# Routed attention and a feed-forward block on one core: 21 of the q and k sides transposed in blocks by VectorE, masks placed by transfers, small chained transfers on GpSimd's queue

## The chip, the cores and the metric

The kernel runs on one core of a Trainium2 chip. TensorE (PE in the profile) multiplies matrices and writes to PSUM, VectorE (DVE) and ScalarE (ACT) compute on SBUF and PSUM, GpSimd (POOL) computes on SBUF and can start transfers, and SyncE (SP) only starts transfers. The metric is the time of one execution on the device, in microseconds. Of the kernel before, five executions are given, with a median of 978.92 us (978.76 to 979.87).

## The reference

Attention with 4 batches, 8 heads, 768 tokens and 64 dimensions a head. Each token of q and of k is assigned to the nearest of 16 centroids of its head, and a query sees only the keys of its own cluster:

```python
q_assign = np.argmax(np.einsum('bhsd,hcd->bhsc', q_n, c_n), axis=-1)
k_assign = np.argmax(np.einsum('bhsd,hcd->bhsc', k_n, c_n), axis=-1)
mask = q_assign[:, :, :, None] == k_assign[:, :, None, :]
scores = scale * np.matmul(q, k.transpose(0, 1, 3, 2))
scores = np.where(mask, scores, -1000000000.0)
```

A softmax over the keys and a product with v follow. The heads are laid side by side into rows of 512, and a feed-forward block comes after: layer norm with a gain, a 512 x 2048 product, a ReLU, a 2048 x 512 product, and the residual. All of it is float32; the weights arrive as float64.

## The kernel before

**Two stages.** The attention stage handles 16 pairs of heads (4 batches x 4 pairs); the feed-forward stage then handles the four batches one after the other with matrix products that are split so that seven products of blocks do the work of eight. The change lies in the attention stage.

**A pair.** A pair's work on TensorE is cut into 12 steps: two halves of 384 queries (`g`) by six blocks of 128 keys (`c`). Two steps make a slot, so a pair has slots 0 to 5. For each step `scores` (L330) puts four matmuls into one PSUM tile: for each head of the pair a matmul of one-hot masks in bf16 (keys' clusters against queries' clusters, where the keys' mask holds 0 for the own cluster and -2^100 elsewhere) and one of k and q in float32. ScalarE then takes the exponential (L341). `weigh` (L353) multiplies it by v into an accumulator (L360), and VectorE adds the exponentials up for the denominators (L374, L377). Scores run a slot ahead of the weighing. There are two PSUM tiles of scores and five SBUF tiles of exponentials.

**Preparing the next pair.** q and k of the pair are loaded with 128 tokens groups on the partitions and must be turned so that the 2 x 64 dimensions lie on the partitions:

- `load` (L76) issues two transfers for a side, one per head, on SP's queue. The tiles `q` and `k` have one buffer each, so that a load starts when the one before has been transposed.
- `prep_transpose` (L236) does six 128 x 128 transposes on TensorE (L243) into two PSUM tiles, which ScalarE copies to SBUF (L249). For pair n+1 the k side is turned in slot 0 of pair n; the q side of pair n+2 is turned in slot 5 of pair n.
- `prep_sims` (L253) in slot 1: similarities to the centroids, copied by ScalarE (L269).
- `prep_turn` and `prep_route` in slot 2: three transposes, then VectorE finds the largest similarity (L285) and writes the one-hot tile (L287).
- `prep_onehot` (L297) in slot 4: six bf16 transposes (L302) into one PSUM tile whose four groups of 32 partitions are q head 0, q head 1, k head 0 and k head 1. Four ScalarE instructions copy each group to its place in `mask[n % 2][side]` (rows 0 to 31 and 64 to 95): a plain copy for q (L316), and FAR * x - FAR for k (L314). The first scores of pair n+1 use these masks in slot 5 of pair n, since scores run ahead.

**Finishing the pair before.** `finish` (L389) has three parts, in slots 1, 3 and 5. Part 0 sums the exponentials over the partitions with a matmul by ones (L397), copies the result to `dsb` (L405), and spreads each of its four rows of 384 over 32 partitions of 12 with four transfers (L407). Part 1 takes the reciprocal on VectorE (L409), stores it to `row` in DRAM (L411) and loads it back as `rb`, each row broadcast over 64 partitions (L419, two transfers that wait for the store). Part 2 multiplies x by rb (L426), stores x (L427), transposes it in 32 x 32 blocks with VectorE (L433), and stores the blocks with four transfers of 128-byte pieces (L436).

**Other work in these slots.** VectorE converts the float64 weights, seven instructions a chunk (L209 to L231): two chunks a pair up to pair 9 (split in slots 0 and 3, joined in slots 1 and 4), then one. In pairs 5 to 8 it takes row statistics of batch 0 (L464, L465), in pair 9 it finishes them, and from pair 10 it applies the norm (L493, L495).

**What sets the order.** The attention loop stands in a block whose instructions on TensorE, VectorE and ScalarE run in the order in which they are written (`manual_schedule`, L562). The order on SP and GpSimd is set by the scheduler, by when it expects each transfer to be ready; a queue issues in order, and a transfer whose input is not there holds up those behind it. In this kernel GpSimd does only memsets and one select at the start. All transfers of the attention loop are on SP.

Of the kernel before, what the change touches and what calls it, by code (L numbers as in the profile page):

```python
# [8 lines left out]
F32 = mybir.dt.float32  # L9
BF16 = mybir.dt.bfloat16  # L10
U32 = mybir.dt.uint32
I32 = mybir.dt.int32
AF = mybir.ActivationFunctionType
# [6 lines left out]
def kernel(  # L20
# [11 lines left out]
    nc = tc.nc  # L32
    B, H, S, D = q.shape
    NCL = centroids.shape[1]
    DM, FF = moe_w_ch1.shape
    P = 128
    NT = S // P
    NHALF = 2
    TH = NT // NHALF
    HC = TH * P  # L40
    Q = 32
# [4 lines left out]
    FAR = 2.0 ** 100  # L46
    WIDE = 1.0e20

    const = ctx.enter_context(tc.tile_pool(name="const", bufs=1))
# [9 lines left out]
    loads = pool("loads", 1)  # L59
    heads = pool("heads", 2)  # L60
    route = pool("route", 1)
    conv = pool("conv", 1)
    attn = pool("attn", 2)
    dram = ctx.enter_context(tc.tile_pool(name="dram", bufs=4, space=bass.MemoryType.DRAM))
# [8 lines left out]
    pairs = [(b, pr) for b in range(B) for pr in range(NPAIR)]  # L73
    loaded = {n: {} for n in range(len(pairs))}

    def load(n, names):  # L76
        if n >= len(pairs):
            return
        b, pr = pairs[n]
        for name in names:  # L80

            shape = [P, 2, NT, D] if name == "v" else [P, NT, 2, D]
            t = loads.tile(
                shape, F32, tag=name, name=f"{name}_sb", bufs=2 if name == "v" else 1
            )

            parts = 1 if n or name == "v" else NHALF
            for g in range(parts):
                cs = slice(g * NT // parts, (g + 1) * NT // parts)
                for j in range(2):  # L90
                    queue = nc.scalar if parts > 1 and j else nc.sync
                    queue.dma_start(
                        out=t[:, j] if name == "v" else t[:, cs, j, :],
                        in_={"q": q, "k": k, "v": v}[name][b, 2 * pr + j].rearrange(
                            "(p c) d -> p c d", p=P
                        )[:, cs, :],
                    )
            loaded[n][name] = t
# [24 lines left out]
    for m in mask[0] + mask[1]:  # L123
        nc.gpsimd.memset(m, 0.0)
    hits = const.tile([P, B * NPAIR], F32, name="hits")
    far = const.tile([P, 1], F32, name="far")
    nc.gpsimd.memset(far, -FAR)

    DE = HC // Q
    rdens = const.tile([P, B * NPAIR, DE], F32, name="rdens")  # L130
# [105 lines left out]
    def prep_transpose(n, side):  # L236
        src = loaded[n]["qk"[side]]
        t_sb = heads.tile([P, S], F32, tag=f"t{side}", name=f"t{side}")
        prepared[n][side] = t_sb
        for g in range(NHALF):  # L240
            t = ps("qk_ps")
            for c in range(TH):
                nc.tensor.transpose(  # L243
                    t[:, c * P : (c + 1) * P],
                    src[:, g * TH + c, :, :].rearrange("p h d -> p (h d)"),
                    ident,
                )
            if g == 0 or n:
                nc.scalar.copy(t_sb[:, g * HC : (g + 1) * HC], t[:, :HC])  # L249
            else:  # L250
                nc.vector.tensor_copy(t_sb[:, g * HC : (g + 1) * HC], t[:, :HC])
# [45 lines left out]
    def prep_onehot(n):  # L297
        t = ps("oh_ps", BF16, 1024)
        for g in range(NHALF):
            for c in range(TH):  # L300
                o = (g * TH + c) * P
                nc.tensor.transpose(  # L302
                    t[:, o : o + P],
                    onehot[:, c, g, :, :, :].rearrange("p s j d -> p (s j d)"),
                    identb,
                )

        for side in range(2):
            m = mask[n % 2][side]
            for j in range(2):  # L310
                src = t[(side * 2 + j) * Q : (side * 2 + j + 1) * Q, :S]
                dst = m[j * D : j * D + Q, :]
                if side:
                    nc.scalar.activation(dst, src, AF.Identity, bias=far[:Q], scale=FAR)  # L314
                else:
                    nc.scalar.copy(dst, src)  # L316
            prepared[n]["m", side] = m

# [69 lines left out]
    def finish(n, part):  # L390
        b, pr = pairs[n]
        if part == 0:
            den = ps("den_ps")
            for j in range(2):
                for g in range(NHALF):
                    r = (j * NHALF + g) * Q
                    nc.tensor.matmul(  # L397
                        den[r : r + Q, :HC], ones, sums[n, g][:, j, :],
                        start=True, stop=True, tile_position=(0, r),
                    )  # L400
            if n + 1 < len(pairs):
                dsb = last.tile([P, HC], F32, tag="dsb", name="dsb", bufs=1)
            else:
                dsb = late["all"][:, 1, :HC]
            nc.scalar.copy(dsb, den[:, :HC])  # L405
            for r in range(0, P, Q):
                nc.sync.dma_start(out=rdens[r : r + Q, n, :], in_=dsb[r : r + 1, :])  # L407
        elif part == 1:
            nc.vector.reciprocal(rdens[:, n, :], rdens[:, n, :])  # L409
            row = dram.tile([2, S], F32, tag="row", name="row")  # L410
            nc.sync.dma_start(  # L411
                out=row.rearrange("j (p e) -> (j p) e", e=DE), in_=rdens[:, n, :]
            )
            if n + 1 < len(pairs):
                rb = last.tile([P, S], F32, tag="rb", name="rb", bufs=1)
            else:
                rb = late["all"][:, 2]
            for j in range(2):
                nc.sync.dma_start(  # L419
                    out=rb[j * D : (j + 1) * D, :],  # L420
                    in_=row[j : j + 1, :].to_broadcast([D, S]),
                )
            late[n] = rb
        else:
            x = xs.pop(n)
            nc.vector.tensor_tensor(x, x, late.pop(n), ALU.mult)  # L426
            nc.sync.dma_start(out=xT_d[b][pr], in_=x)  # L427

            if n + 1 < len(pairs):
                y = last.tile([P, S], F32, tag="y", name="y")  # L430
            else:
                y = late["all"][:, 2]
            nc.vector.transpose(y, x)  # L433
            for i in range(P // Q):
                m = pr * P + i * Q
                nc.sync.dma_start(  # L436
                    out=x_d[b].rearrange("t (a r) m -> r (t a) m", r=Q)[:, :, m : m + Q],
                    in_=y[i * Q : (i + 1) * Q].rearrange("r (g f) -> r g f", f=Q),
                )
# [4 lines left out]
    rows = {}  # L444
# [117 lines left out]
    with tc.manual_schedule(engines=order):  # L562
        prep_transpose(0, 0)
        load(1, "q")
        turn_centroids()
        prep_transpose(0, 1)
        load(1, "k")
        prep_sims(0)
        scores(0, "qk", ("qk",))
        prep_turn(0)  # L570
        scores(1, "qk", ("qk",))
        prep_route(0)
        prep_transpose(1, 0)
        load(2, "q")
        load_weight(0)
        load_weight(1)
        prep_onehot(0)
        scores(0, "qk", ("mask", "exp"))
        scores(1, "qk", ("mask", "exp"))
        for u in range(len(pairs) * slots):  # L580
            n, slot = divmod(u, slots)
            nxt = n + 1 < len(pairs)
            if slot == 1:
                load(n + 1, "v")
            if slot == 0 and nxt:
                prep_transpose(n + 1, 1)
                load(n + 2, "k")
            if slot == 1 and nxt:
                prep_sims(n + 1)
            if slot == 2 and nxt:  # L590
                prep_turn(n + 1)
                prep_route(n + 1)
            if slot == 4 and nxt:
                prep_onehot(n + 1)
            if slot == 5 and n + 2 < len(pairs):
                prep_transpose(n + 2, 0)
                load(n + 3, "q")
            if slot == 1 and n:
                finish(n - 1, 0)
            for i in (2 * u + 2, 2 * u + 3):  # L600
                if i < len(steps):
                    scores(i)
            weigh(2 * u)
            weigh(2 * u + 1)
            if slot == 3 and n:
                finish(n - 1, 1)
            if slot == 5 and n:
                finish(n - 1, 2)
            if (n, slot) in convert:
                split_weight(convert[n, slot])  # L610
            if (n, slot - 1) in convert:
                join_weight(convert[n, slot - 1])
                load_weight(convert[n, slot - 1] + 2)
            for job in extra.pop((n, slot), ()):
                job()
# [446 lines left out]
```

## Time and profile before

| | us |
|---|---|
| median of five executions | 978.92 |
| the profiled execution | 979.14 |
| its span | 977.4 |
| TensorE busy | 954.6 (98%) |
| VectorE busy | 640.3 (66%) |
| ScalarE busy | 329.7 (34%) |
| a pair of the attention stage, from pair 1 on | 23.37 |
| TensorE busy in it | 23.00 |

The profile is of one execution. Its page gives busy times and shares, the chain of work that ended last (followed back from the last instruction to what released each step), groups of equal instructions by source line, and the transfers. Queries of the trace give one stretch of time, the waits of an engine, or the instructions in order. A line of a group reads: source line, engine, operation, output<-input, shapes, count, then busy us and mean ns of one, then the idle time of the engine before them and what ended it. A line of a stretch gives its start and end, its length, each engine's busy us with the number of instructions, TensorE's granted clock, the share of the DMA engines and GB/s. A line of the chain gives start, length and what ran; "issue" is time in which nothing that is shown was waited for. Lines with SPq are transfers being issued by SP's queue.

### The profile page before, as it was taken

Reading aid. Unit: us, or ns where it says so; the run is one execution under the profiler, and the core shown is the slowest. Engines: PE = TensorE matmul, PEld = TensorE weight load, DVE = VectorE, ACT = ScalarE, POOL = GpSimd, SP = SyncE. Lnnn points to the kernel's source line nnn. Section 1 sums busy time; section 2 is a strip of 40 time slices with the busy share of each in tenths; the row PEclk is TensorE's granted clock in tenths of the full one; section 3 lists DMA queues with packets and bytes.
Section 4 is the critical chain, followed back from the end, with each engine's and each line's share of the span. In section 5 each row is a group of like instructions: output and inputs, shape, how many; then the busy total and the mean of one; then the engine's idle time right before and its main releaser. Section 6 shows DMA issues by size and latency. Waiting matters only on the chain.

```text
span 977.4 us, 12727 instructions
## 1 busy us (share of the span) xinstructions
PE 954.6 (98%) x4758; PEld 593.3 (61%) x4758; DVE 640.3 (66%) x1206; ACT 329.7 (34%) x525; POOL 4.9 (1%) x31
## 2 busy tenths in 40 slices
PE   5999999999999999999999999999999999999997
PEld 3444444444444443556888556888556888556886
DVE  2788888998877777799874455653455564455431
ACT  4667676677676676222000221000211000221000
POOL 2000000000000000000000000000000000000000
PEclk9999999999999999999999999999999999999999
DMA  6346656665654422432542000212000221000011
GB/s 158 98 119 165 169 159 189 165 167 156 157 137 119 119 74 59 113 98 75 172 120 71 6 0 1 97 60 71 0 1 6 92 71 60 1 1 6 28 39 40
DMA packets 141445, 84.01 MB, mean 86 GB/s; under 512 B 110608, under 2 KB 127040, under 8 KB 141376
## 3 DMA queue, kind: packets, MB, share of 16 engines
q1 hardware_dynamic: 139104, 82.70, 30.7%
q8 instruction: 39, 0.64, 0.3%
q10 hardware_dynamic: 2272, 0.43, 0.2%
q14 instruction: 30, 0.25, 0.1%
HBM read 64.00 MB, written 19.00 MB: 85 GB/s over the span
## 4 chain that ended last, share of the span: by engine, by line
PE 90%; ACT 5%; issue 2%; DMA 1%; DVE 1%; ACTq 0%; SPq 0%; DVEq 0%
PE x_ps L737 17%; PE x_ps L652 17%; PE s_ps L348 14%; PE a_ps L360 12%; PE z_ps L737 8%; PE z_ps L652 8%; PE y_ps L737 4%; PE y_ps L652 4%; ACT mask_0k L314 1%; ACT mask_1k L314 1%; PE qk_ps L243 1%; ACT e L341 1%; PE sim_ps L260 1%; PE den_ps L397 1%; DMA q_sb<-in_q_dram 1%
## 5 line engine op out<-in xcount | busy, mean ns | idle before, releaser
L341 ACT ACTIVATE e<-s_ps 128x768 f32<-128x768 f32 x192 | 151.8, 817 | 55.1 <-PE s_ps L348 53.1
L348 PE MATMUL s_ps<-t,t 64*128 64x384 f32 x768 | 156.5, 486 | 0.0
L377 DVE TENSOR_TENSOR es<-es,e 128x768 f32<-128x768 f32 x128 | 122.3, 955 | 38.8 <-ACT e L341 32.2
L360 PE MATMUL a_ps<-e,v_sb 128*64 128x384 f32 x768 | 144.8, 499 | 0.0
L360 PEld LDWEIGHTS a_ps<-e,v_sb 128*64 128x64 f32 x768 | 46.7, 136 | 86.5 <-issue 86.3
L737 PE MATMUL x_ps<-w2t,h 128*128 128x256 f32 x384 | 84.5, 379 | 0.0
L348 PEld LDWEIGHTS s_ps<-t,t 64*128 64x128 f32 x768 | 69.3, 190 | 19.6 <-issue 19.4
L737 PEld LDWEIGHTS x_ps<-w2t,h 128*128 128x128 f32 x384 | 72.7, 190 | 10.1
L667 ACT COPY u<-x_ps 128x384 f32<-128x384 f32 x64 | 30.7, 479 | 134.2 <-PE x_ps L652 134.2
L667 ACT COPY p<-x_ps 128x384 f32<-128x384 f32 x32 | 15.3, 479 | 139.3 <-PE x_ps L652 139.3
L530 DVE TENSOR_TENSOR ws<-w 128x256 f32<-128x256 f32 x64 | 24.8, 418 | 53.3 <-PE z_ps L652 53.3
L748 DVE TENSOR_TENSOR o_sb<-x_ps,xb 128x256 f32<-128x256 f32 x48 | 20.1, 420 | 54.9 <-PE x_ps L737 54.9
L672 DVE TENSOR_TENSOR h<-z_ps,u 128x384 f32<-128x384 f32 x64 | 35.2, 550 | 22.4 <-ACT u L667 13.8
L652 PE MATMUL x_ps<-xn,w 128*128 128x384 f32 x128 | 46.6, 487 | 0.6 <-ACT late L386 0.6
L652 PE MATMUL z_ps<-xt,ws 128*128 128x384 f32 x128 | 46.6, 487 | 0.0
L652 PE MATMUL x_ps<-xt,w 128*128 128x384 f32 x128 | 46.6, 487 | 0.0
L652 PE MATMUL z_ps<-xn,ws 128*128 128x384 f32 x128 | 46.5, 486 | 0.0
L652 PE MATMUL y_ps<-xn,w 128*128 128x384 f32 x128 | 46.5, 486 | 0.0
L652 PE MATMUL x_ps<-xt,ws 128*128 128x384 f32 x128 | 46.5, 486 | 0.0
L652 PE MATMUL x_ps<-xn,ws 128*128 128x384 f32 x128 | 46.5, 486 | 0.0
L737 PE MATMUL x_ps<-w,h 128*128 128x256 f32 x192 | 42.7, 379 | 0.0
L737 PE MATMUL y_ps<-w,h 128*128 128x256 f32 x192 | 42.1, 379 | 0.0
(130 smaller groups left out, 1309.2 us busy)
## 6 DMA issues: line engine op xcount, KB each, us to landing
raw<-in_moe_w_ch_dram SPq DMA_DIRECT2D x32, 512.0 KB, 3.9
v_sb<-in_v_dram SPq DMA_DIRECT2D x32, 192.0 KB, 4.0
xn<-xT_d SPq DMA_DIRECT2D x16, 384.0 KB, 4.8
xr<-x_d SPq DMA_DIRECT2D x24, 256.0 KB, 3.0
xb<-x_d SPq DMA_DIRECT2D x48, 128.0 KB, 2.2
out_dram<-o_sb SPq DMA_DIRECT2D x48, 128.0 KB, 1.7
q_sb<-in_q_dram SPq DMA_DIRECT2D x30, 192.0 KB, 4.1
k_sb<-in_k_dram SPq DMA_DIRECT2D x30, 192.0 KB, 3.7
```

Source lines behind the costliest of these rows:

```text
L243: nc.tensor.transpose(t[:, c * P : (c + 1) * P], src[:, g * TH + c, :, :].rearrange("p h d -> p (h d)"), ident,)
L314: nc.scalar.activation(dst, src, AF.Identity, bias=far[:Q], scale=FAR)
L341: nc.scalar.activation(e, s[:, :, :HC], AF.Exp, scale=SCALE)
L348: nc.tensor.matmul(s[:, j, :HC], of_keys[rows[j], keys], of_queries[rows[j], cols], start=part == first, stop=part != first, skip_group_ch ...
L360: nc.tensor.matmul(acc[j * D : (j + 1) * D, :HC], loaded[n]["v"][:, j, c, :], e[:, j, :], start=(c == 0), stop=(c == NT - 1),)
L377: nc.vector.tensor_tensor(es, es, soft.pop(i), ALU.add)
L530: nc.vector.tensor_tensor(t[:, i], x, y, op)
L652: nc.tensor.matmul(bank[:, :HC], lhs[:, c, :], rhs[:, c, :], start=first and c == 0, stop=c == NDH - 1, skip_group_check=True,)
L667: nc.scalar.copy(t, bank[:, :HC])
L672: nc.vector.tensor_tensor(h, bank[:, :HC], other, ALU.add)
L737: nc.tensor.matmul(bank[:, :MH], hidden[lhs + (c,)][:, tt * P : (tt + 1) * P], rhs[:, c, :], start=first and c == 0, stop=c == NFH - 1, sk ...
L748: nc.vector.tensor_tensor(o, bank[:, :MH], x, ALU.add)
```

## The change

**Block transposes.** For the k sides of pairs 1 to 15 and the q sides of pairs 10 to 15, 21 sides in all, the load places 32 x 32 blocks so that VectorE's transpose, which turns each 32 x 32 block in place, gives the whole transposed side. One VectorE instruction (128 x 768, float32) replaces six TensorE transposes and two ScalarE copies. Such a load is four transfers on SP's queue, one for each 32 dimensions, with 128-byte pieces. The other 11 sides stay as they were.

**Masks.** One ScalarE instruction with a bias and a scale per partition (0 and 1 for the q rows, -FAR and FAR for the k rows) writes all 128 rows to a tile `m`; four transfers on GpSimd's queue bring 16 rows of 768 each to their places in the masks. `prep_onehot` moves from slot 4 to slot 3.

**Chained transfers.** The spreading of the denominators becomes a store to DRAM (`flat`) and a load from it, and these two, the store of `row` and the two loads of `rb` go to GpSimd's queue. SP keeps the loads and the other stores.

```diff
+    blocks = {(n, name) for n in range(1, len(pairs)) for name in ("qk" if n >= 10 else "k")}
+
+    def load_blocks(n, name):
+        b, pr = pairs[n]
+        t = loads.tile([P, S], F32, tag=name, name=f"{name}_sb")
+        for i in range(P // Q):
+            nc.sync.dma_start(
+                out=t[i * Q : (i + 1) * Q].rearrange("f (t a r) -> f t a r", t=NT, r=Q),
+                in_={"q": q, "k": k}[name][b, 2 * pr + i * Q // D].rearrange(
+                    "(a f t) d -> f t a d", f=Q, t=NT
+                )[:, :, :, i * Q % D : i * Q % D + Q],
+            )
+        loaded[n][name] = t
...
+            if (n, name) in blocks:
+                load_blocks(n, name)
+                continue
...
-    far = const.tile([P, 1], F32, name="far")
-    nc.gpsimd.memset(far, -FAR)
+    far = const.tile([P, 2], F32, name="far")
+    for rows, bias, scale in ((slice(0, D), 0.0, 1.0), (slice(D, P), -FAR, FAR)):
+        nc.gpsimd.memset(far[rows, 0:1], bias)
+        nc.gpsimd.memset(far[rows, 1:2], scale)
...
+        if (n, "qk"[side]) in blocks:
+            nc.vector.transpose(t_sb, src)
+            return
...
+        m = route.tile([P, S], BF16, tag="m", name="m")
+        nc.scalar.activation(m, t[:, :S], AF.Identity, bias=far[:, 0:1], scale=far[:, 1:2])
         for side in range(2):
-            m = mask[n % 2][side]
             for j in range(2):
-                src = t[(side * 2 + j) * Q : (side * 2 + j + 1) * Q, :S]
-                dst = m[j * D : j * D + Q, :]
-                if side:
-                    nc.scalar.activation(dst, src, AF.Identity, bias=far[:Q], scale=FAR)
-                else:
-                    nc.scalar.copy(dst, src)
-            prepared[n]["m", side] = m
+                o = (side * 2 + j) * Q
+                nc.gpsimd.dma_start(
+                    out=mask[n % 2][side][j * D : j * D + NCL, :], in_=m[o : o + NCL, :]
+                )
+            prepared[n]["m", side] = mask[n % 2][side]
...
-            for r in range(0, P, Q):
-                nc.sync.dma_start(out=rdens[r : r + Q, n, :], in_=dsb[r : r + 1, :])
+            flat = dram.tile([P // Q, HC], F32, tag="flat", name="flat")
+            nc.gpsimd.dma_start(out=flat, in_=dsb[0:P:Q, :])
+            nc.gpsimd.dma_start(
+                out=rdens[:, n, :], in_=flat.rearrange("i (p e) -> (i p) e", e=DE)
+            )
...
-            nc.sync.dma_start(
+            nc.gpsimd.dma_start(
                 out=row.rearrange("j (p e) -> (j p) e", e=DE), in_=rdens[:, n, :]
             )
...
-                nc.sync.dma_start(
+                nc.gpsimd.dma_start(
                     out=rb[j * D : (j + 1) * D, :],
                     in_=row[j : j + 1, :].to_broadcast([D, S]),
                 )
...
-            if slot == 4 and nxt:
+            if slot == 3 and nxt:
                 prep_onehot(n + 1)
```

## The prediction

> **What bounds the kernel now.** I read the page's busy table first, then one row per head pair of the attention stage, then the chain of work and the waits inside one pair, then the groups of the operations that the change touches.
>
> ```profile
> PE 954.6 (98%) x4758; PEld 593.3 (61%) x4758; DVE 640.3 (66%) x1206; ACT 329.7 (34%) x525; POOL 4.9 (1%) x31
> ```
> ```profile
> core 0: us, PE busy (x) PEld busy (x) DVE busy (x) ACT busy (x) POOL busy (x), PEclk, DMA share, GB/s
> ...
> 111.98:135.35 23.37, 23.00 (x157) 10.36 (x157) 19.71 (x31) 16.23 (x25) 0.00 (x0) 1.00 0.61 165
> ...
> 182.10:205.47 23.37, 23.00 (x157) 10.37 (x157) 21.24 (x35) 16.24 (x25) 0.00 (x0) 1.00 0.67 170
> ...
> 275.59:298.97 23.37, 23.00 (x157) 10.36 (x157) 17.78 (x25) 16.23 (x26) 0.00 (x0) 1.00 0.51 126
> ```
> TensorE is the bound. Every pair takes 23.37 us and TensorE is busy for 23.00 of them at a granted clock of 1.00. VectorE comes second: 19.7 us in a plain pair, 21.2 us where pairs 5 to 8 also do the row statistics. GpSimd does nothing in this stage. The FFN stage after 390 us is not touched, so I set its change at zero: its chain is matmuls whose inputs this change does not move.
>
> The chain of pair 5, then the waits behind it:
>
> ```profile
> 137.15 1.44 PE a_ps L360 x8
> 138.59 0.81 PE qk_ps L243 x6
> 139.39 1.72 PE s_ps L348 x12
> ...
> 156.03 0.90 ACT mask_0k L314
> 156.92 0.03 issue
> 156.95 0.90 ACT mask_0k L314
> 157.84 0.02 issue
> 157.87 0.82 ACT e L341
> 158.69 0.04 issue
> 158.73 1.45 PE s_ps L348 x9
> ```
> A slot (two steps) is 1.72 us of scores and 1.44 us of weighing, 3.16 us, and what else TensorE does adds to it. Six transposes of a k side are 0.81 us on the chain. Late in the pair the chain leaves TensorE: four mask copies keep ScalarE from the exponential, and the next scores start late. The timeline shows 0.37 us of idle TensorE there, which is the pair's 23.37 less 23.00.
>
> ```profile
> L433 DVE STREAM_TRANSPOSE y<-x 128x768 f32<-128x768 f32 x15 | 14.7, 978 | 0.5
> L314 ACT ACTIVATE mask_0k<-oh_ps,far 32x768 bf16<-32x768 bf16 x16 | 14.3, 895 | 0.3
> ```
> ```profile
> 139.27 3.33 SPq L436 DMA_DIRECT2D x_d<-y  x4
> 142.69 1.25 SPq L92 DMA_DIRECT2D k_sb<-in_k_dram  x2
> 145.20 2.47 SPq L407 DMA_DIRECT2D rdens<-dsb  x4
> 151.79 0.32 SPq L411 DMA_DIRECT2D row<-rdens  x1
> 154.01 1.13 SPq L419 DMA_DIRECT2D rb<-row  x2
> ```
> The first group prices the new VectorE transpose, the second the new mask copy: 32 or 128 partitions, the same 768 columns. The issue rows price a transfer: 0.32 us to 0.83 us of its queue (3.33 over 4). A dependent transfer starts 2.22 us after its source began issuing (151.79 to 154.01), so about 1.9 us after the issue ends.
>
> **The change part by part.** Sums are made against the profiled execution, 979.14 us (span 977.4 and 1.7 around it), 0.2 us above the median of 978.92.
>
> *TensorE transposes out.* The k sides of pairs 1 to 15 and the q sides of 10 to 15 make 21, each 0.81 us of the chain: **-17.0 us**. Two ScalarE copies of 0.49 us go with each; they are off the path.
>
> *Mask copies.* Four of 0.79 to 0.90 us become one of about 0.9. ScalarE's 3.4 us between 154.43 and 157.84 shrink to 0.9 and move a slot earlier, in front of an exponential that waited 0.44 us for its scores anyway. The 0.37 us stall goes at 15 pairs: **-5.5 us**. A plain pair is then 22.16 us on TensorE, and 21.35 us from pair 8, where slot 5 loses the q transposes of pair 10. I count from the start of slot 0; slots 1 to 5 then begin at 3.16, 7.77, 11.40, 15.02 and 18.18 us.
>
> *Masks in time?* The one-hot transposes end at 11.86, the mask copy at about 12.83. The reciprocal is ready at 12.5, so the row transfer probably goes ahead of four mask transfers on GpSimd's queue. With I for the issue of one transfer, the last mask lands at 12.5 + 5I + 1.9. TensorE wants it at 18.18, or at 18.99 where q transposes still come first (pairs 0 to 7). No row shows a transfer issued by GpSimd. From the rows of SP, I lies between 0.32 and 0.83; nothing excludes more, so for the upper end I take 1.2, about half above the dearest row. [...] That gives 18.55: nothing in pairs 0 to 7, 0.36 us late in the seven others: **+2.5 us** (0 at 0.32).
>
> *The first pair has no cover.* Its masks were done at 20.32 us by ScalarE. Now the copy ends at 17.93, and 4 x 0.83 + 1.9 later it is 23.15; TensorE resumed at 20.38: **+2.8 us** (0.7 at 0.32, 4.2 at 1.2).
>
> *VectorE's load.* A plain pair costs VectorE 23.37 less its waits (1.74 for simT, 1.16 for e), 20.5 us, now 21.4 with a transpose of 0.95 start to start. That fits 22.16 alone. Row statistics add 0.8 each (two in pairs 6 and 7, one in 5 and 8), q sides 0.95 from pair 8. Queued behind the new transpose are the sums and the weight conversion; waiting for it are the similarity matmuls at 3.16, which it meets if VectorE reaches it by 2.1. The multiplication by rb is the other end: row lands at 15.2, rb goes after the masks at 16.65, its second half lands near 21.3 (3.3 us by its median), and VectorE would be there at 20.2. So in plain pairs VectorE is 1.0 us behind at the next slot 0, inside the 2.1. From pair 5 the lag grows by what the pair costs over TensorE's time: 1.8, 2.7, 3.0, 3.9 and 3.1 at the starts of pairs 6 to 10. Each excess over 2.1 stops TensorE once and resets that much: 0.6, 0.9, 1.8 and 1.0: **+4.3 us** (0 if the sums can slide further, 8 if the lag reaches the one-hot as well). After pair 10 half the weight conversions are gone and it recovers.
>
> *Queues.* SP loses 2.47 + 0.32 + 1.13 = 3.9 us of issue a pair. A block load is four transfers of 128-byte pieces like the x_d stores, so about 3.33 us in place of 1.25: +2.1 a side. SP's issues of pair 5 add up to 13.4 us; that becomes 11.6, and 13.6 with both sides. A block load is issued once its predecessor is transposed and is used a pair later, with some 6 us of issue and landing against 20. I cost it at nothing; without that cover VectorE's transpose, then the similarities, would wait. 1536 more pieces a side at 34.5 ns (30.7% of 16 engines' span over 139104 packets) are at most 3.3 us of the 16 engines, a share of 0.61 going to 0.75, and 0.51 to 0.8 with two sides. The two chained transfers of the denominators start at 5.1 (ScalarE's copy) and take 2 x (0.83 + 1.9), 10.6: before the reciprocal at 12.3.
>
> The sum: -17.0 - 5.5 + 2.5 + 2.8 + 4.3 = -12.9, so **966.2 us**.
>
> [...]
>
> **The rivals.**
> - *GpSimd's issue becomes the bound (ends slower).* Lateness is 8 x (5I - 4.59) + 7 x (5I - 3.78), the first pair adds 4I - 0.7, and VectorE's lag hides in the stalls. Against -22.5 that breaks even at I = 1.08; at 1.2 the time is 988. For it: seven transfers in one stretch of under 6 us, on a queue with none before. Against it: no issue row reaches 0.84 except where it was queued. If the masks go ahead of the row instead, rb lands late by the same amount and VectorE passes it on.
> - *VectorE is the bound in all of pairs 0 to 9.* One microsecond a pair more (a late rb, GpSimd in its way) makes 22.4 against 22.16; the excess less the slack is then about 9 us in place of 4.3: 971. For it: the 21.4 is already 97% of the pair. Against it: its two waits gave 2.9 us of room.
> - *All of it hides.* I near 0.32 and a VectorE lag that costs nothing: 979.1 - 22.5 + 0.7 + 1 = 958. Against it: pair 8 needs 23.2 us of VectorE in 21.35.
>
> **How the numbers follow.** My forecast has 0.42, the GpSimd bound 0.30, VectorE 0.15, all hidden 0.13. Leaving out a tenth at each end, the range is 958 to 989; the forecast's own is 962 to 971. About 0.2% (2 us) is what a measurement here can tell from no change: faster 0.65, the same 0.06 (I between 1.05 and 1.11, out of the GpSimd case and the upper edge of VectorE's), slower 0.29.
>
> **What would show it.** Right: pairs of about 22.2 us, then 21.4; no idle before the first scores of a pair; one transpose of 0.98 us for each of 21 sides. Wrong: scores that wait for a transfer into the masks at slot 5; GpSimd issues over 1.08 us; x waiting for rb by more than 2 us; similarities waiting for the transpose in plain pairs; block loads that land after VectorE wants them; less than 2 us lost in the first pair.

## The result and the profile after

The changed kernel takes 983.6 us in the median of 23 executions (977.92 to 991.98); the kernel before, beside it, 979.24 us in 43 (978.01 to 980.45). The ratio is 1.0044, with a 95% interval of 1.0033 to 1.0054: **slower by 0.4%**, where the prediction had it 13 us faster. Its executions spread over 14 us against 2.4 before, and the profiled one, with 987.86 us and a span of 986.1, lies 4 us above the median. So a single late transfer in it is read with care, and the sizes below come from medians where they can. Executions more than 1.5% above the fastest of the same kernel are left out of every ratio.

The busy table of after; then three stretches of one pair's length (columns as in the table of before): from slot 5 of pair 1 to slot 5 of pair 2, and from slot 1 of pairs 6 and 10 to slot 1 of the next pair.

```profile
PE 949.7 (96%) x4632; PEld 582.0 (59%) x4632; DVE 659.5 (67%) x1227; ACT 277.5 (28%) x435; POOL 81.3 (8%) x178
```
```profile
core 0: us, PE busy (x) PEld busy (x) DVE busy (x) ACT busy (x) POOL busy (x), PEclk, DMA share, GB/s
65.79:87.92 22.13, 22.13 (x152) 9.53 (x153) 18.82 (x30) 13.25 (x19) 4.82 (x9) 1.00 0.65 161
...
162.40:191.66 29.26, 25.28 (x156) 10.44 (x159) 26.41 (x41) 13.25 (x19) 4.78 (x9) 0.88 0.63 156
258.45:289.12 30.67, 24.12 (x149) 10.14 (x153) 23.52 (x34) 12.45 (x17) 4.70 (x9) 0.89 0.81 154
```

A plain pair is what the change was to make of it: 22.13 us, and TensorE is busy for all of them. TensorE lost 126 matmuls (4758 to 4632), which is 21 x 6. Two pairs are 7 and 9 us too long, with TensorE idle *and* at a lower clock. What TensorE waited for in the whole run, and VectorE's largest new wait (us in total, times, longest):

```profile
PE s_ps L370 <- DMA mask_1k<-m: 11.7, 5, 6.6
PE s_ps L370 <- DMA mask_0k<-m: 5.6, 2, 5.2
PE sim_ps L283 <- DVE t L261: 4.8, 3, 4.0
...
DVE x L451 <- DMA rb<-row: 24.1, 7, 5.9
```

None of the four existed before. (L370 are the scores, L283 the similarities, L261 the new VectorE transpose, L451 the multiplication by rb.) The sum over the attention stage shows where the loss lies. With no stall, by the shortest pairs of the runs here and with the first pair and the last stretch of experiment 9, the feed-forward stage would start at 25.7 + 21.5 + 7 x 22.12 + 6 x 21.32 + 37.9 = 367.9 us. In before it starts at 390.9, so the promised gain is there: 23.0 us, and 22.5 were forecast. In after it starts at 399.9:

| lost against 367.9, in the profiled execution | us |
|---|---|
| first pair: scores wait for the masks | 3.5 |
| pair 6 to 7: similarities wait for VectorE, which waited for rb | 7.1 |
| pair 10 to 11: scores wait for the masks | 9.4 |
| pair 14 to the end of the stage: scores wait for the masks, behind a gap of 2.9 us on GpSimd's queue | 6.5 |
| seven other pairs, 0.2 to 1.7 each | 5.5 |

The feed-forward stage itself is unchanged: 586.2 us against 586.5.

**Pair 10.** GpSimd's queue in a plain pair, and in this one (start, length, what was issued, how long it stood before and for what):

```profile
105.42 0.54 POOL L436 DMA_DIRECT2D row<-rdens  x1 [4.57 <-DVE ta L229]
105.97 1.08 POOL L336 DMA_DIRECT2D mask_0q<-m  x2
107.04 0.96 POOL L336 DMA_DIRECT2D mask_0k<-m  x2
108.06 1.05 POOL L444 DMA_DIRECT2D rb<-row  x2
...
270.75 0.55 POOL L436 DMA_DIRECT2D row<-rdens  x1 [5.00 <-DVE rdens L434]
274.43 0.53 POOL L444 DMA_DIRECT2D rb<-row  x1 [3.14 <-DMA row<-rdens]
274.99 1.04 POOL L336 DMA_DIRECT2D mask_1q<-m  x2
276.02 0.96 POOL L336 DMA_DIRECT2D mask_1k<-m  x2
```

One issue takes about 0.53 us, less than the 0.83 taken. But in pair 10 the masks, copied by 268.70, are issued at 274.99: they stand behind row, which waits for VectorE's reciprocal, and behind one of the two rb transfers, which waits until row has landed. The chain there, and the granted clock after it:

```profile
270.75 3.16 DMA row<-rdens
...
276.02 4.49 DMA mask_1k<-m
...
280.55 3.84 PE s_ps L370 x12
```
```profile
274.00:280.50 6.50, 0.00 (x0) 0.00 (x0) 1.39 (x2) 0.00 (x0) 3.00 (x6) 0.79 0.91 136
280.50:284.40 3.90, 3.85 (x14) 1.88 (x16) 2.93 (x4) 0.81 (x1) 0.00 (x0) 0.50 0.28 102
284.40:287.70 3.30, 3.30 (x22) 1.40 (x24) 3.06 (x5) 2.06 (x3) 0.00 (x0) 0.97 0.87 134
```

TensorE stands still for 6.5 us and then runs at a clock of 0.50 for 3.9 us, which is another 2 us: the twelve matmuls of scores take 3.84 us there, and 1.72 in the chain of before. From 284.40 the clock is 0.97.

**Pair 6** is another story. Row, issued at 150.48, took 4.7 us to land (its median is 1.7), so that rb stood for 2.65 us on GpSimd's queue (first line, of that queue); then rb itself took 7.0 us to land (156.25 to 163.27). VectorE stood at x, and the transpose of the next k side, two instructions behind it, came late for the similarities (the chain):

```profile
155.72 1.05 POOL L444 DMA_DIRECT2D rb<-row  x2 [2.65 <-DMA row<-rdens]
```
```profile
156.25 7.01 DMA rb<-row
...
163.36 0.97 DVE x L451
...
166.12 0.99 DVE t L261
...
167.15 0.85 PE sim_ps L283 x2
```

That makes three readings. **Q**: the masks share an in-order queue with transfers that wait. **V**: VectorE has too much to do in pairs 5 to 10. **L**: the chained transfers land late, VectorE stands at x, and what is queued behind x is late.

### The profile page after: what moved, and what is told of

It reads as the page before. It is cut to its first block, busy times and chain, and to the rows that moved or that the text cites. A ratio compares the mean times of both kernels' runs of the same rounds, so it can differ in the third digit from the quotient of the medians.

```text
span 986.1 us, 12594 instructions
## 1 busy us (share of the span) xinstructions
PE 949.7 (96%) x4632; PEld 582.0 (59%) x4632; DVE 659.5 (67%) x1227; ACT 277.5 (28%) x435; POOL 81.3 (8%) x178
## 4 chain that ended last, share of the span: by engine, by line
PE 85%; DMA 5%; issue 4%; DVE 3%; POOL 1%; ACT 1%; SPq 0%; ACTq 0%; POOLq 0%; DVEq 0%
PE x_ps L762 17%; PE x_ps L677 17%; PE s_ps L370 13%; PE a_ps L382 10%; PE z_ps L762 8%; PE z_ps L677 8%; PE y_ps L762 4%; PE y_ps L677 4%; DMA q_sb<-in_q_dram 2%; PE sim_ps L283 1%; PE den_ps L419 1%; DMA mask_1k<-m 1%; DMA row<-rdens 1%; DMA rb<-row 1%; PE qk_ps L266 1%
## 5 line engine op out<-in xcount | busy, mean ns | idle before, releaser
L370 PE MATMUL s_ps<-t,t 64*128 64x384 f32 x768 | 161.8, 497 | 0.0
L370 PEld LDWEIGHTS s_ps<-t,t 64*128 64x128 f32 x768 | 71.4, 194 | 23.1 <-issue 23.1
L370 PE MATMUL s_ps<-mask_1q,mask_1k 64*128 64x384 bf16 x192 | 34.5, 335 | 11.7 <-DMA mask_1k<-m 11.7
```

The costliest lines, as they stand in the source:

```text
L370: nc.tensor.matmul(s[:, j, :HC], of_keys[rows[j], keys], of_queries[rows[j], cols], start=part == first, stop=part != first, skip_group_ch ...
```

## The experiments

Each ratio is against the kernel before on the same chip, with its 95% interval. "Tenth pair" means pair 10.

**1. row and rb back on SP.**

```diff
-            nc.gpsimd.dma_start(
+            nc.sync.dma_start(
                 out=row.rearrange("j (p e) -> (j p) e", e=DE), in_=rdens[:, n, :]
...
-                nc.gpsimd.dma_start(
+                nc.sync.dma_start(
                     out=rb[j * D : (j + 1) * D, :],
```

> Theory Q (the masks stand in GpSimd's queue behind the row transfer, which waits for VectorE's reciprocal): with row and rb on SP, the masks go out as soon as they are copied; the waits of TensorE for masks after the first pair (6.6, 3.1 and 1.7 us in the profile of the changed kernel) are gone, with the slow clock that follows them, and the time falls from 983.6 to about 968. Theory V (VectorE is overloaded by the transposes in pairs 5 to 10): the waits for masks turn into waits for the transposed k or q sides, and the time stays within 978 to 984. Theory L (chained transfers land late among the block loads): rb still lands 4 to 7 us after its issue, VectorE still waits some 20 us for it in all, and the time is 974 to 982.

Measured: 996.77 us, 1.0171 (1.0154 to 1.0187). The mask waits are gone after the first pair, as Q says, but the time is worse. Waits of this kernel:

```profile
DVE x L451 <- DMA rb<-row: 40.1, 13, 4.1
...
PE sim_ps L283 <- DVE t L261: 22.0, 10, 3.8
```

Why rb is late there is seen on SP's queue in pair 6:

```profile
183.44 0.34 SPq L436 DMA_DIRECT2D row<-rdens  x1
...
189.30 0.33 SPq L220 DMA_DIRECT2D raw<-in_moe_w_ch_dram  x1
189.73 1.13 SPq L444 DMA_DIRECT2D rb<-row  x2
```

Between row and rb stands a load of weights that waits for VectorE to free its buffer (such loads hold SP for 81.9 us in 24 waits). From row to rb pass 3.7 to 8.2 us in ten pairs running, in before 1.4 to 2.7. So Q's mechanism moved to another queue and came back as L; taking the chain off GpSimd alone can't show the price of Q.

**2. Blocks alone.** The kernel before with the block loads and VectorE's transposes; masks and queues as before.

```diff
+            if (n, name) in blocks:
+                load_blocks(n, name)
+                continue
...
+        if (n, "qk"[side]) in blocks:
+            nc.vector.transpose(t_sb, src)
+            return
```

> The kernel before with the 21 block loads and VectorE transposes alone; masks by ScalarE in slot 4 and all transfers on SP as before. Theory V: the similarities wait for VectorE's transposes in pairs 5 to 10 as in the changed kernel, and the time is 975 to 984. Theory Q: TensorE keeps most of the 17 us, 964 to 968, since the masks wait for no transfer; the 0.37 us stall of each pair stays. Theory L: in between, 966 to 975, with VectorE waiting for rb on SP, where it now stands behind block loads.

Measured: 1058.01 us, 1.0807 (1.0789 to 1.0825), by far the slowest. Its SP queue:

```profile
305.43 1.12 SPq L219 DMA_DIRECT2D raw<-in_moe_w_ch_dram  x1
318.26 0.36 SPq L111 DMA_DIRECT2D v_sb<-in_v_dram  x1
318.84 0.33 SPq L433 DMA_DIRECT2D row<-rdens  x1
```

The reciprocal had ended at 308.89; row stands ten microseconds behind a load of v that waits for TensorE to finish with its buffer. VectorE waits for rb for 78.0 us in 11 times (up to 10.0), TensorE for the transpose for 59.6. It is the same head-of-line wait as in Q, on the other queue, and far larger: the kernel is 78.7 us slower than before. With the order that SP's queue has here, the blocks lose more than they gain while the chain stays on SP; another order on SP was not tried.

**3. No blocks: masks and chain alone.**

```diff
-    blocks = {(n, name) for n in range(1, len(pairs)) for name in ("qk" if n >= 10 else "k")}
+    blocks = set()
```

> The changed kernel without any block load or VectorE transpose (all sides on TensorE); masks by transfers, chain on GpSimd's queue. Theory V and theory L: VectorE has its 2.9 us of room in a pair again and the queue of loads is short, so nothing stalls after the first pair; 5.5 us are won by ScalarE, some 5 lost in the first pair with its slow clock, 976 to 980. Theory Q alone, without VectorE being late, says the same; if the row waits long enough to hold the masks even here, 982 to 990.

Measured: 977.42 us, 0.9978 (0.9969 to 0.9988). Plain pairs take 22.93 us, 0.44 under the 23.37 of before, where 0.37 were the stall behind ScalarE's copies. TensorE keeps its transposes, so every pair has VectorE time to spare; there are mask waits only in the first pair (4.43 us idle) and at pair 14 (1.67). VectorE waits for rb here too, 13.1 us in the six pairs from pair 10 on, and yet pairs 10 to 13 take 22.93 us: a late rb alone costs TensorE nothing there.

**4. The first pair's masks by ScalarE, as before.** All else as in after.

```diff
+        if n == 0:
+            for side in range(2):
+                for j in range(2):
+                    o = (side * 2 + j) * Q
+                    dst = mask[0][side][j * D : j * D + Q, :]
+                    if side:
+                        nc.scalar.activation(
+                            dst, t[o : o + Q, :S], AF.Identity, bias=far[D : D + Q, 0:1], scale=FAR
+                        )
+                    else:
+                        nc.scalar.copy(dst, t[o : o + Q, :S])
+                prepared[n]["m", side] = mask[0][side]
+            return
```

> The changed kernel with the first pair's masks copied by ScalarE as before. The wait of 5.2 us for the first masks becomes about 3.3, as before, and the slow clock behind it (0.55 from 24 to 29 us) comes back to 0.75 or so: 4 to 5 us less than the changed kernel, about 979, if that loss stands by itself; no change if it is absorbed later.

Measured: 977.13 us, 0.9974 (0.9956 to 0.9993), 6.6 us under after, each against before on its own chip. By the two profiles, the similarities in slot 1 of pair 1 start at 47.33 us in place of 50.72, so 3.4 us come from the first pair. The attention stage ends 16.5 us earlier than in the profile of after, at 383.4 in place of 399.9. The pair that began with a late rb in after takes 23.35 us in place of 29.26. And at pair 14 the gap of 2.9 us on GpSimd's queue moved: in after it stands ahead of the masks, here, with four transfers fewer in the first pair, four issues later, behind them (GpSimd's queue of after, then of this kernel):

```profile
367.99 0.55 POOL L436 DMA_DIRECT2D row<-rdens  x1 [6.84 <-DVE rdens L434]
371.47 1.05 POOL L336 DMA_DIRECT2D mask_1q<-m  x2 [2.93 <-ACT e L363]
```
```profile
357.89 0.55 POOL L449 DMA_DIRECT2D row<-rdens  x1 [6.85 <-DVE rdens L447]
358.44 1.04 POOL L349 DMA_DIRECT2D mask_1q<-m  x2
...
363.31 1.05 POOL L457 DMA_DIRECT2D rb<-row  x2 [2.88 <-issue]
```

So the gain is more than the first pair's: the gap no longer stands ahead of masks. Of these 16.5 us the feed-forward stage gives back 5.9, in the way that experiment 5 shows below, and the profile of after lies 4 above its median. The tenth pair still takes 31.17 us, with a mask wait of 5.88.

**5. As 4, rb issued behind the next pair's masks.**

```diff
-                nc.gpsimd.dma_start(
+                placed[n] = nc.gpsimd.dma_start(
                     out=mask[n % 2][side][j * D : j * D + NCL, :], in_=m[o : o + NCL, :]
...
+            with ExitStack() as after:
+                if n + 2 in placed:
+                    after.enter_context(tc.issue_after(placed[n + 2].ins))
                 for j in range(2):
                     nc.gpsimd.dma_start(
                         out=rb[j * D : (j + 1) * D, :],
```

> The kernel of e4_first_pair with rb always behind the masks in GpSimd's queue; so far one pair, the tenth, has half of rb ahead of them. Theory Q: that one order costs 9.8 us (a pair of 31.2 us where 21.4 would do, most of it the wait for the masks and the half clock after it), so 977.1 becomes 967 to 969. Theory V: VectorE is late in that pair whatever the order, and TensorE waits for its transposes instead: 972 to 977. Theory L: rb, now a little later, makes VectorE wait more: 970 to 977.

Measured: 974.35 us, 0.9951 (0.9934 to 0.9969). The tenth pair falls from 31.17 to 23.55 us, its mask wait from 5.88 to 1.43: the transfer put in front of the masks was the cause of that pair. The whole gains only about 3 us over experiment 4. The waits for rb are as they were (19.2 us, 18.7 in experiment 4), and experiment 9 shows that it is now they that set the time. The end of the attention stage shows where they go (VectorE in order, then TensorE):

```profile
365.42 0.96 DVE L468 TENSOR_TENSOR x<-x,rb 128x768 f32<-128x768 f32 x1 [5.56 <-DMA rb<-row]
...
384.54 0.96 DVE L468 TENSOR_TENSOR x<-x,rb 128x768 f32<-128x768 f32 x1 [2.55 <-DMA rb<-row]
...
386.44 0.38 DVE L572 TENSOR_TENSOR ws<-w 128x256 f32<-128x256 f32 x1
```
```profile
387.43 2.90 PE L694 MATMUL x_ps<-xt,ws 128*128 128x384 f32 x4 [3.03 <-DVE ws L572]
```

VectorE waits 5.6 us (2.9 of them are the gap on GpSimd's queue), then 2.6 us; the weight sums for the feed-forward stage come behind x and y, and TensorE waits 3.0 us for them and runs at 0.50 until 390 us. That stage takes 591.2 us here, 4.6 more than in before.

**6. As 4, row and rb both behind the masks.**

```diff
+            with ExitStack() as after:
+                if n + 2 in placed:
+                    after.enter_context(tc.issue_after(placed[n + 2].ins))
                 nc.gpsimd.dma_start(
                     out=row.rearrange("j (p e) -> (j p) e", e=DE), in_=rdens[:, n, :]
                 )
```

> The kernel of e4_first_pair with row and rb both behind the masks in every pair. Theory Q in its wide form (the masks suffer from the row transfer's wait for VectorE in many pairs): at or below e5_rb_after_masks, with no wait of TensorE for a mask, 965 to 968. Theory L: row goes out some 2 us later in plain pairs, rb lands that much later, VectorE waits for it in most pairs: 970 to 978. Theory V: as in e5.

Measured: 981.29 us in the median of seven executions (975.41 to 988.3; three more took 991.16 to 997.79), 1.0024 (0.999 to 1.0058). In the profiled one, of 979.3 us, TensorE hardly waits for a mask (0.6 us in all), but VectorE waits 28.5 us for rb, up to 7.1 at a time. So Q is not cured by putting the masks first: the chain of row and rb has no time to give.

**7. As 4, with the k sides of pairs 6 to 10 back on TensorE.**

```diff
+        for name in ("qk" if n > 10 else "q" if n == 10 else "" if n > 5 else "k")
```

> The kernel of e4_first_pair without the k blocks of pairs 6 to 10 (16 sides left; in this kernel, too, the scheduler puts rb behind the masks everywhere). Theory V: VectorE has room in the pairs with the row statistics, nothing waits there, and though TensorE takes back 5 x 0.81 = 4.1 us the time is at or below that of e5: 966 to 969. Theory Q: it is e5 plus about 4 us, 971 to 973.

Measured: 973.76 us, 0.9953 (0.9935 to 0.9971); experiment 5 of the same chip is at 974.35. (Here the scheduler put rb behind the masks by itself.) TensorE takes back five sides, 4.1 us, and the time does not change: in those pairs VectorE's lag eats what TensorE gains. That is V, and about 4 us of it.

**8. As 4, with plain loads of two transfers and 256-byte pieces in place of the block loads.**

```diff
-        for i in range(P // Q):
+        for j in range(2):
             nc.sync.dma_start(
-                out=t[i * Q : (i + 1) * Q].rearrange("f (t a r) -> f t a r", t=NT, r=Q),
...
+                out=t.rearrange("p (c h d) -> p c h d", c=NT, h=2)[:, :, j, :],
+                in_={"q": q, "k": k}[name][b, 2 * pr + j].rearrange("(p c) d -> p c d", p=P),
```

> The kernel of e4_first_pair with the 21 sides still turned by VectorE but loaded as before in two transfers of 256-byte pieces, so the values that are turned are wrong and only the time is read (here, too, rb stands behind the masks in every pair). Theory L, with the 128-byte block loads as what delays the chained transfers: the hops of flat, rdens, row and rb take about 2.2 us in place of 3 and more, VectorE's waits for rb (18.7 us in e4) nearly vanish, and the time is 4 us or more below e5. Theories Q and V: within 1.5 us of e5.

Measured: 972.34 us, 0.9928 (0.991 to 0.9946), 2.0 us under experiment 5. VectorE still waits 18.9 us for rb (19.2 there). The small pieces of the block loads, with the two further issues a side, cost about 2 us and are not what makes the chain late.

**9. As 5, with x, y and the store one slot later**: part 2 of `finish` moves from slot 5 to slot 0 of the next pair, so that rb has more time to land; the sums go ahead of it on VectorE.

```diff
-            if slot == 5 and n:
+            if slot == 0 and n > 1:
+                finish(n - 2, 2)
+            if slot == 5 and n + 1 == len(pairs):
                 finish(n - 1, 2)
```

> The kernel of e5_rb_after_masks with the last part of the finish (x times rb, its transpose and stores) moved from slot 5 to slot 0 of the next pair, some 4 us later; nothing else in it changes. Theory L (the chain of row and rb takes 7 to 8 us from the reciprocal, and in pairs 9 to 14 VectorE has only about 5 us of other work between): VectorE's waits for rb, 19.2 us in six pairs, vanish but for the last pair's, and the pairs from the tenth on, 22.3 to 24.1 us each in e5, come down to 21.4 to 22.3: 974.4 becomes 966 to 970. Theory V (VectorE is simply full): the same work is done a little later, the similarities wait as before, and the time is within 1.5 us of e5.

Measured: **964.74 us** (964.13 to 965.68), 0.9855 (0.9839 to 0.9872). It beats both kernels. Its page, and its wait for rb:

```profile
PE 939.0 (98%) x4632; PEld 578.6 (60%) x4632; DVE 658.4 (68%) x1227; ACT 279.3 (29%) x438; POOL 79.4 (8%) x174
```
```profile
DVE x L468 <- DMA rb<-row: 2.1, 3, 1.0
```

With most of 19.2 us of waits gone, the median falls by 9.6 us. Between the two profiles it is 10.4: 5.8 before the feed-forward stage starts and 4.6 in it. The last pairs take 21.37, 21.32 and 21.32 us: the 21.35 of the forecast. What is left over the shortest pairs is 4.4 us from pair 5 to pair 10 (V, 4.3 forecast) and 3.4 us at pair 10, where the masks still wait behind row.

**10. As 9, with the k sides of pairs 6 to 10 back on TensorE.**

```diff
+        for name in ("qk" if n > 10 else "q" if n == 10 else "" if n > 5 else "k")
```

> e9_x_later without the k blocks of pairs 6 to 10 (16 sides). TensorE takes back 5 x 0.81 = 4.1 us. If VectorE's load in the pairs with the row statistics still costs the 4 us that the prediction gave it, this is equal to e9; if e9 has removed that as well, it is 3 to 4 us slower than e9.

Measured: 964.81 us, 0.9857 (0.9837 to 0.9877), the same as experiment 9: with L and most of Q gone, too, the blocks of these pairs are worth nothing.

**11. After, with nothing but the later x.**

```diff
-            if slot == 5 and n:
+            if slot == 0 and n > 1:
+                finish(n - 2, 2)
+            if slot == 5 and n + 1 == len(pairs):
                 finish(n - 1, 2)
```

> The changed kernel with nothing but the last part of the finish moved to slot 0 of the next pair. Theory L: the late landings of rb, one of which costs the profiled execution 7 us in the sixth pair, reach TensorE no more; the first pair's loss stays: 968 to 974, and the executions spread over 4 us or less where the changed kernel's spread over 14. Theory Q: the pair in which rb stands ahead of the masks, if it still does, keeps its 9 us: 975 to 979.

Measured: 986.49 us, 1.0066 (1.0043 to 1.0088). The waits for rb are gone here too, yet there is no gain. The scheduler now puts both rb transfers ahead of the masks in five pairs (GpSimd's queue, then TensorE):

```profile
241.62 0.55 POOL L436 DMA_DIRECT2D row<-rdens  x1 [6.69 <-DVE ta L229]
243.59 1.06 POOL L444 DMA_DIRECT2D rb<-row  x2 [1.43 <-DMA row<-rdens]
244.64 1.12 POOL L336 DMA_DIRECT2D mask_0q<-m  x2
```
```profile
248.19 0.33 PE L370 MATMUL s_ps<-mask_0q,mask_0k 64*128 64x384 bf16 x1 [2.71 <-DMA mask_0k<-m]
```

These pairs take 24.0 to 28.0 us. This shows Q by itself: the same move that is worth 9 us where rb stands behind the masks is worth nothing where it stands ahead of them.

**12. Before, with nothing but the later x.**

```diff
-            if slot == 5 and n:
+            if slot == 0 and n > 1:
+                finish(n - 2, 2)
+            if slot == 5 and n + 1 == len(pairs):
                 finish(n - 1, 2)
```

> The kernel before with the same move. There VectorE waits for no rb and TensorE is the bound, so by every theory the time stays at 979, within 1 us; if it falls by more, the move has a value of its own that e9 owes nothing to the change for.

Measured: 979.22 us, 0.9999 (0.9989 to 1.0009). In the kernel before, x did not wait for rb, and the later x is worth nothing. Experiment 9's gain belongs to the wait that the change brought.

Each kernel less the one before of the same chip, in us: after +4.4; first pair's masks by ScalarE -2.2; rb behind the masks -5.2; x later -14.3.

## Why the prediction was wrong

The forecast was 966.2 us, by a sum of -12.9; after measured +4.4, 17.3 us more. Experiments 4, 5 and 9 take 6.6, 3.0 and 9.1 us off in turn. By the steps of the forecast:

- **TensorE transposes out, -17.0, and mask copies, -5.5: right.** The stage without stalls is 23.0 us shorter for a sum of 22.5; plain pairs take 22.13 us (22.16 forecast), later ones 21.32 (21.35). The row for y<-x priced the transpose well:

```profile
L261 DVE STREAM_TRANSPOSE t<-k_sb 128x768 f32<-128x768 f32 x15 | 14.4, 958 | 3.2 <-DMA k_sb<-in_k_dram 3.2
...
L332 ACT ACTIVATE m<-oh_ps,far 128x768 bf16<-128x768 bf16 x16 | 15.9, 992 | 0.0
L336 POOL DMA_DIRECT2D mask_1k<-m x16 | 7.7, 485 | 0.0
```

- **"VectorE's load ... +4.3": right in size, but not by the wait that was named.** Experiment 9 shows 4.4 us in pairs 5 to 10, and experiments 7 and 10 that TensorE's five sides there buy nothing. But in experiment 9 the similarities never wait for VectorE's transpose; TensorE waits for the one-hot tiles that VectorE writes, 2.4 us in four times, a way that the term had mentioned and not priced in. That the size fits is partly luck.
- **"Queues ... I cost it at nothing": right for the loads** (about 2 us, experiment 8).
- **"Masks in time? ... +2.5": the step that failed, and not by its price.** Issues by GpSimd take 0.48 to 0.60 us by their means, not 0.83, and with that the formula gives no loss outside the first pair. But the formula let row go out 12.5 us after the start of slot 0, with a reciprocal that is never late, and put nothing but row's issue ahead of the masks. On this in-order queue the masks also take over what the transfers in front of them wait for. In pair 10 the reciprocal ended at 15.2 us, and one rb, which waits for row's landing, went ahead of the masks as well: they were issued 6.3 us after they were copied. The pair lost 9.4 us in the profiled execution, and experiment 5, with rb behind the masks, shortens it by 7.6. No value of I describes this, and I had let I carry the whole uncertainty: the rival that ended slower had the sign, but its condition, an I above 1.08, was not met. (By its own terms it breaks even at 1.09, since the first pair adds 4I - 0.55; nothing hangs on that.)
- **"The first pair has no cover ... +2.8": right in kind, 3.4 to 3.5 measured.** The masks came sooner than priced: TensorE restarted at 21.83 in place of 23.15, only 1.45 us later than in before. But it had idled 5.2 us, and the sum had no term for the clock (from TensorE's restart on). In before the clock was 0.55 from 20.38 to 24.00 and 1.00 behind it, so that after loses some 1.8 us more to it (an estimate from these clocks):

```profile
21.83:24.00 2.17, 1.59 (x7) 0.50 (x8) 0.00 (x0) 1.14 (x2) 0.00 (x0) 0.50 0.50 79
24.00:29.20 5.20, 5.20 (x20) 1.96 (x18) 4.40 (x7) 2.00 (x3) 0.00 (x0) 0.55 0.00 0
```

- **"After pair 10 half the weight conversions are gone and it recovers": wrong, the second step that failed, and by the medians the larger.** In before VectorE came to x 8.2 to 9.1 us after the reciprocal, in every pair but the last, and rb was there. In plain pairs of after it comes at 7.9 us and rb is there; the price of the chain, landing 9.0 us after the reciprocal, was even too high. But from pair 10 on VectorE, with less to do, would be at x after 4.4 to 6.7 us, and rb, which goes behind four masks, is there after 7.4 to 7.9, or 10 to 11 in pairs 10 and 14. So it stands there in every one of these pairs (VectorE's rows in pairs 12 and 13):

```profile
329.73 0.96 DVE L451 TENSOR_TENSOR x<-x,rb 128x768 f32<-128x768 f32 x1 [2.76 <-DMA rb<-row]
...
352.30 0.96 DVE L451 TENSOR_TENSOR x<-x,rb 128x768 f32<-128x768 f32 x1 [2.22 <-DMA rb<-row]
```

  I had compared rb with VectorE in a plain pair only, and let pairs 11 to 15 be free. With x a slot later (experiment 9) VectorE starts x 8.3 to 10.8 us after the reciprocal in pairs 10 to 14, and that is worth 9 to 10 us against experiment 5. Half of it lies in the feed-forward stage, whose change I had set "at zero": that holds for after itself (586.2 us), but not for experiments 4 and 5.
- **The price of an issue, 0.83: too high.** The sums of the masks and of the first pair take it from the dearest row of SP; no run shows it for an issue of GpSimd. The 144 issues of GpSimd in after take 0.53 us in the mean and 0.63 at most. The queues do differ: the store of row is issued in 0.33 us by SP (before and experiment 1) and in 0.55 by GpSimd (after), and lands 1.4 and 1.7 us after its issue; rb is issued in 0.59 and 0.53 us and lands after 3.3 (before) and 3.6 (after). Issues of GpSimd differ among themselves, too: in after one for a q mask took 0.57 to 0.61 us where a one-input operation of the conversion ran beside it (ten issues) and 0.48 to 0.51 beside two-input ones (15). What that 0.1 us comes from, no run took apart.

What stays open. Why row and then rb landed so late in one pair of the profiled execution: a load of q and one of weights had been issued just before rb, and the DMA engines' busy share was 0.9 and more from 156.2 to 162 us, but no run took this apart. Nor is it known how much of the spread of after comes from such landings. And the gap of 2.9 us at pair 14: it is there in after and in experiments 3 to 5 and 7 to 11, each time behind the 128th transfer that GpSimd issues, whichever comes next. In experiment 1, where GpSimd issues 96 transfers, there is none. So it goes with the count of GpSimd's issues and not with what the transfers wait for; the "ACT e" in the row of after is no cause. What the gap is, no run took apart.

## What to carry to other kernels

When a transfer moves to another queue, write down for each transfer on it what it waits for, and charge that wait to everything issued behind it (the masks of pair 10 stood 6.3 us); a price per issue is not enough. When a change takes work off the bound, follow the engine that had no time to wait before: with time in hand it reaches its waits early. A consumer moved one slot later can be worth more than the change itself (here 9 us of 979, and nothing in the kernel that lacked the wait).

## What the runs showed of the hardware

Neither queue issued both transfers of the chain faster: the store of row took 0.33 us on SP (before) and 0.55 on GpSimd (after), the two loads of rb 0.59 and 0.53 each. Behind the 128th transfer that GpSimd issued, the profiles of nine kernels show a gap of 2.9 us, whose cause is open. And two stalls of TensorE in after cost more than their length: the granted clock was 0.50 for 3.9 us after the wait of 6.5 us in pair 10, which is 2 us of work, and 0.50 to 0.55 for 7.4 us after the one of 5.2 us in the first pair, some 3.4 us of work (before lost 1.6 in its first pair as well).
